# Moving the softmax normalisation, the weight conversions and one pre-addition inside an attention loop

## The chip, the cores and the metric

The kernel runs on one core of a Trainium2 chip. The metric is the device time of one execution in microseconds (us). TensorE (PE) multiplies, VectorE (DVE) and ScalarE (ACT) work elementwise, and most transfers are issued in order from the queue of SyncE (SP).

## The reference, cut to what matters

An attention with capped scores for 4 batches of 12 heads (448 tokens of 64 elements) is followed by a dense layer pair with squared ReLU (768 to 2048 to 768) on the 1792 tokens, and by a layer that sends each token to one of 8 experts.

```python
scores = scale * np.matmul(q, k.transpose(0, 1, 3, 2))
scores = cap * np.tanh(scores / cap)
scores = scores - np.max(scores, axis=-1, keepdims=True)
attn = np.exp(scores)
attn = attn / (np.sum(attn, axis=-1, keepdims=True) + 1e-09)
attn_out = np.matmul(attn, v)

h = x @ w_in            # x: 1792 x 768, from attn_out
r = np.maximum(h, 0.0)
x = (r * r) @ w_out
...
h = np.maximum(x[mask] @ w1[e], 0.0)      # per expert e
out[mask] = gate_w[mask, None] * (h @ w2[e])
```

## The kernel before, in words

The order of the work is written out by hand: each engine runs its instructions in the order in which the program emits them, and semaphores hold it where an operand or a buffer is not ready.

**Attention** (`attention`, L131) treats two heads at a time, a pair. There are 24 pairs and a loop of 25 periods (`pr` = 0 to 24, L297). In period `pr` TensorE computes the transposed scores of pair `pr` in three chunks of 128 keys (`scores`, L185), the values of the pair before (`values_last` L228, `values` L235 and L244), and the last 64 keys of the next pair (`scores_last`, L200), which ends the period on TensorE. ScalarE takes tanh of each score chunk (L191, L205) and exp of a pair in one instruction (L211), and copies the odd head's result out of PSUM (L253). VectorE does four kinds of things in a period, in this order: `fold` (L219), which adds exponentials of the pair before, chunk on chunk, into a tile `W`; the steps that are hung on the even index `i = 2*pr` (the middle slot); `prep` (L61 and L63), which splits the queries and keys of pair `pr + 2` into a high and a low part; `copy_out` of the even head (L256); and the steps that are hung on `i + 1` (the end slot).

**The row sums** come from matmuls with a matrix of ones (L244): one matmul for each head and each part, where the parts are `W` and the chunks that were not added into it. With `chunks = 2`, chunks 0 and 1 are added by one VectorE instruction and chunk 2 has ones matmuls of its own; with `chunks = 3` a second VectorE instruction adds chunk 2, and its matmuls fall away. Before, `chunks` is 3 in odd periods up to 15 and 2 elsewhere.

**The normalisation** goes over groups `u` of four heads (two periods). `norm_sum` (L274, L276) has SP send the row sums of a finished pair to a small tile `den` and then move the odd head's values into place (`x<-ot`), which must wait until the `den` transfer has read what it overwrites. `norm_recip` (L336, L337) takes the reciprocal on VectorE, `norm_spill` (L341) has SP write it to DRAM (`dd`), `norm_spread` (L349) has SP read it back, broadcast to all partitions (`r`, two transfers of 224 KB), and `norm_x` (L356) multiplies on VectorE, one instruction for each of the group's two pairs. The list `when` (L283) says at which index, counted from `i0 = 4u + 6`, each of the five steps is hung. An odd index is the end slot of a period, an even one the middle slot.

**The weights** for the first blocks of the dense layers come as 64-bit floats and are converted by VectorE in steps (`w_steps`, L445): three chunks, six VectorE steps each, of three kinds (begin, middle, end), plus two loads of 384 KB a chunk on SP's queue. Before, they hang on the indices 4, 5, 8, 9, 12, 13 and so on, two in every even period from 2 on. `split_x` (L403) splits group 0's normalised tokens for the first dense layer, one of six parts at each of six listed indices.

SP's queue takes in each period, in order: `qkraw` of pair `pr + 4` (L164, after `prep` has freed its buffer), the two `den` transfers, `x<-ot`, `v` (L170), and what the slots hang on it. Buffers: two for `qkraw`, `hl`, `W`, `r` and `den`, three for `ot`, four for `v`; in PSUM three for scores and two for values.

**At the start** SP loads the first queries and keys in two parts, then `cap`, values and the next pair. **After attention** the dense layers (`moe1`) and the experts (`moe2`) follow; from there on TensorE has work nearly all the time.

Of the kernel before, what the change touches and what calls it, by code (L numbers as in the profile page):

```python
# [21 lines left out]
NHD = B * H  # L22
# [12 lines left out]
FOLD_ALL = 32  # L35
FB = 2
NU = 4
# [11 lines left out]
class Kernel:  # L49
# [16 lines left out]
    def constants(self):  # L66
        nc, tc = self.nc, self.tc
        p = self.const
        cap = p.tile([128, 1], F32, name="cap")
        nc.sync.dma_start(out=cap, in_=self.a["cap"].rearrange("(o n) -> o n", o=1).to_broadcast([128, 1]))  # L70
        self.cap = cap

    def scales(self):
# [57 lines left out]
    def attention(self, tail_p):  # L131

        nc, tc, a = self.nc, self.tc, self.a
        with ExitStack() as ctx:
# [8 lines left out]
            ps_s = pool("pss", 3, space=PSUM)  # L143
            ps_o = pool("pso", 2, space=PSUM)

            z, y = self.ring["o"][0][0][:, :512], self.const.tile([128, 1], F32, name="y")
            nc.gpsimd.memset(y, 0.0)
            nc.scalar.activation(out=y, in_=y, func=ACTF.Tanh)
# [10 lines left out]
            def load(pr, cuts=(0, QK)):  # L159
                if pr < NP:  # L160
                    b, j = divmod(pr, H // 2)
                    raws[pr] = raw_p.tile([128, QK], F32, tag="qk", name="qkraw")
                    for c0, c1 in zip(cuts, cuts[1:]):
                        nc.sync.dma_start(out=raws[pr][:, c0:c1], in_=a["qk"][b, j, :, c0:c1])  # L164

            def load_v(pr):
                if pr < NP:
                    b, j = divmod(pr, H // 2)
                    vs[pr] = v_p.tile([KP, 2 * KC, D], F32, tag="v", name="v")
                    nc.sync.dma_start(out=vs[pr], in_=a["v"][b, j])  # L170
# [38 lines left out]
            def exps(pr):  # L209
                t = P[pr]  # L210
                nc.scalar.activation(out=t, in_=t, func=ACTF.Exp, scale=self.cap[:KP])  # L211

            def fold(pr, chunks):

                if chunks > 1:
                    W[pr] = w_p.tile([KP, 2, S], F32, tag="w", name="w")
                    src = P[pr][:, 0:2]
                    for c in range(1, chunks):
                        nc.vector.tensor_tensor(out=W[pr], in0=src, in1=P[pr][:, 2 * c:2 * c + 2], op=ALU.add)  # L219
                        src = W[pr]  # L220
# [36 lines left out]

            cuts = (0, S + KP, QK)
            load(0, cuts)
            self.constants()  # L260
            load_v(0)
            load(1)
            load_v(1)
# [16 lines left out]
            last = NHD // NU - 2  # L280
            for u in range(last + 1):
                i0 = NU * (u + 1) + 2
                when = (1, 1, 2, 5, 6)  # L283
                for j, f in zip(when, (
                    lambda u=u: self.norm_recip(den[u]),
                    lambda u=u: dd.update({u: self.norm_spill(den[u])}),
                    lambda u=u: r.update({u: self.norm_spread(n_p if u < last else tail_p, dd[u])}),
                    lambda u=u: self.norm_x(u, r[u], (0,)),
                    lambda u=u: self.norm_x(u, r[u], (1,)),
                )):  # L290
                    if u < last or j < 3:
                        steps.setdefault(i0 + j, []).append(f)


# [1 line left out]
            prep(1)  # L296
            for pr in range(NP + 1):  # L297
                i = 2 * pr
                chunks = 3 if pr % 2 == 1 and i < FOLD_ALL else 2
                if pr:  # L300
                    fold(pr - 1, chunks)
                for c in range(KC - 1):
                    if pr and c == KC - 2:
                        values_last(pr - 1)
                    if pr < NP:
                        scores(pr, c)
                    if not pr and not c:
                        scores_last(pr)
                if pr < NP:
                    exps(pr)  # L310
                if pr:
                    values(pr - 1, chunks)
                    copy_out(pr - 1, 1)
                scores_last(pr + 1)
                for f in steps.get(i, []) + self.side.get(i, []):
                    f()
                prep(pr + 2)
                if pr:
                    copy_out(pr - 1, 0)
                    if pr % 2:  # L320
                        p, bufs = (tail_p, 1) if pr == NP - 1 else (n_p, 2)
                        den.append(p.tile([128, NU * S // 128], F32, tag="den", name="den", bufs=bufs))
                else:
                    load(3)
                load(pr + 4)
                if pr:
                    norm_sum(i - 2)
                    norm_sum(i - 1)
                load_v(pr + 2)
                for f in steps.get(i + 1, []) + self.side.get(i + 1, []):  # L330
                    f()
# [429 lines left out]
def build(ctx, tc, a, stop=None):  # L761
    k = Kernel(ctx, tc, a)
    nc = tc.nc
    pool = lambda name, bufs=1, **kw: ctx.enter_context(tc.tile_pool(name=name, bufs=bufs, **kw))

    def xhl(p, g):
        n = GROUPS[g][1]
        k.xh[g] = p.tile([128, KD, n], F32R, name=f"xh{g}")
        k.xl[g] = p.tile([128, KD, n], F32R, name=f"xl{g}")

    with tc.manual_schedule():
        k.const = pool("const")
        k.cv_p = tc.alloc_tile_pool(name="cv", bufs=4, side="right")
        xp = tc.alloc_tile_pool(name="x", bufs=1, side="right")
        k.x = xp.tile([128, KD, NT], F32, name="x")
        k.raw_p = pool("wraw", 3)
        k.ring, k.used = {"i": [], "o": []}, {"i": 0, "o": 0}
        k.open_weights(pool("w0"), {"i": FB, "o": 1})
        k.xh, k.xl = [None] * NG, [None] * NG
        xhl(pool("x0"), 0)  # L780
        k.moe1_start()
        k.dram = pool("adr", 2, space=DRAM)
        tail_p = tc.alloc_tile_pool(name="tail", bufs=1, side="right")
        side = k.side = {6: [k.gate_loads]}
        at = iter([i for i in range(NU, NHD) if i % NU in (0, 1)])
        chunks = [k.w_steps(*c) for c in (("i", 0), ("i", 1), ("o", 0))]
        side[2] = [chunks[0][0]]
        for n, (_, *rest) in enumerate(chunks):
            for m, f in enumerate(rest):
                i = next(at)  # L790
                side.setdefault(i, []).append(f)
                if m == len(rest) // 2 and n + 1 < len(chunks):
                    side[i].append(chunks[n + 1][0])
        for j, i in enumerate((34, 35, 38, 39, 42, 43)):
            side.setdefault(i, []).append(lambda j=j: k.split_x(0, "dve", "dve", j))
        conv = k.w_conv(*k.chunk(0))
        side.setdefault(43, []).append(lambda: k.w_load(*k.chunk(0)))
        side[NHD] = [lambda: next(conv)]
        k.attention(tail_p)
        k.open_weights(pool("w1", reuse_waits="tile"), {"i": 1, "o": FB})  # L800
        x1 = pool("x1", reuse_waits="tile")
        for g in (1, 2, 3):
            xhl(x1, g)
        k.gt_p = pool("gt", reuse_waits="tile")
        with ExitStack() as c1:
            gp = c1.enter_context(tc.tile_pool(name="g", bufs=4, reuse_waits="tile"))
            k.g_p = gp
            k.ps_h = pool("psh", 3, space=PSUM, reuse_waits="tile")
            k.ps_y = pool("psy", 3, space=PSUM, reuse_waits="tile")
            k.ps_m = pool("psm", 2, space=PSUM, reuse_waits="tile")  # L810
            for j in range(KD):
                k.split_x(1, "act", "dve", j)
            late = {}

            def first():
                k.norm_recip(k.den_last)
                late["r"] = k.norm_spread(tail_p, k.norm_spill(k.den_last), "r2")
                for _ in conv:
                    pass
                k.w_split(*k.chunk(0))  # L820

            def second():
                k.norm_x(NHD // NU - 2, k.r_last)
                k.norm_x(NHD // NU - 1, late["r"])
                tail_p.release()
                for j in range(KD):
                    k.split_x(2, "act", "dve", j)

            k.moe1({(0, 0): first, (1, 0): second})
        xp.release()  # L830
        k.cv_p.release()
        k.h2_p = pool("h2")
        k.w2_p = pool("w2", 6)
        k.out_p = pool("o", 2)
        k.moe2()
        k.other_experts()
# [44 lines left out]
```

## Time and profile before

| | |
|---|---|
| median of 3 runs | 928.44 us (925.5 to 928.48) |
| profiled execution | 929.95 us, of which 928.2 us are the span from the first to the last instruction |
| PE, DVE, ACT busy | 97%, 62%, 40% of the span |
| mean granted TensorE clock | 0.986 |
| attention | about the first 193 us of the span |

A share of the span says little for a stage: attention, the dense layers and the experts load the engines differently. The attention's end is where the first matmul of the dense layer (L413) starts. Its periods can be counted on TensorE by the starts of L200, one per period.

### The profile page before, as it was taken

The numbers are of one execution on the slowest core, as the hardware profiler recorded it, in microseconds if no ns is written. First come the engines' busy times: TensorE is split into PE (matmuls) and PEld (weight loads), VectorE is DVE, ScalarE is ACT, GpSimd is POOL, SyncE is SP. The second block draws the span as 40 slices with busy tenths as digits, with TensorE's granted clock in tenths as the row PEclk, the third lists the DMA queues.
The fourth block names the chain that finished last, engine by engine and source line by source line (L and its number), as shares of the span: only waits on it lengthen the run. The fifth ranks groups of instructions, "written<-read, shape, count | busy, mean of one in ns | idle before, by whom it ended". The sixth has DMA issues, their size and how long they took to land.

```text
span 928.2 us, 12168 instructions
## 1 busy us (share of the span) xinstructions
PE 900.4 (97%) x4678; PEld 742.7 (80%) x4679; DVE 574.6 (62%) x1119; ACT 371.0 (40%) x532; POOL 0.8 (0%) x10
## 2 busy tenths in 40 slices
PE   8999899999999999999999999997889999999997
PEld 5555454568989889898898988986777998999997
DVE  5777586567857667676676766545566536426461
ACT  7999888956533223232232322334221111111111
POOL 0000000000000000000000000000000000000000
PEclk9999999999999999999999999999879999999999
DMA  5454555532312111121111211000114434526451
GB/s 196 136 166 116 170 150 145 150 105 60 101 51 67 53 52 53 50 68 52 52 56 47 68 51 35 1 1 0 58 46 120 119 115 124 156 83 171 136 162 47
DMA packets 39572, 83.30 MB, mean 90 GB/s; under 512 B 8656, under 2 KB 16976, under 8 KB 39504
## 3 DMA queue, kind: packets, MB, share of 16 engines
q1 hardware_dynamic: 35472, 76.92, 28.5%
q10 hardware_dynamic: 4032, 5.51, 1.6%
q8 instruction: 39, 0.64, 0.3%
q14 instruction: 29, 0.24, 0.1%
HBM read 73.97 MB, written 5.59 MB: 86 GB/s over the span
## 4 chain that ended last, share of the span: by engine, by line
PE 89%; DVE 5%; ACT 2%; DMA 2%; issue 1%; SPq 0%; DVEq 0%; ACTq 0%
PE h L413 12%; PE h L414 12%; PE h L415 12%; PE y L413 8%; PE y L415 8%; PE y L414 8%; PE o L235 5%; PE s L185 5%; PE o L413 4%; PE o L415 4%; PE o L414 4%; PE o L244 3%; PE o L228 2%; PE s L200 2%; DMA den<-ot 1%; DVE xl L63 1%
## 5 line engine op out<-in xcount | busy, mean ns | idle before, releaser
L413 PE MATMUL h<-xh,wih 128*128 128x512 f32 (+1 forms) x576 | 211.4, 367 | 0.0
L414 PE MATMUL h<-xl,wih 128*128 128x512 f32 (+1 forms) x576 | 210.6, 366 | 0.0
L415 PE MATMUL h<-xh,wil 128*128 128x512 f32 (+1 forms) x576 | 210.5, 365 | 0.0
L504 DVE TENSOR_TENSOR x<-y,x 128x512 f32<-128x512 f32 (+1 forms) x168 | 104.2, 623 | 72.3 <-PE y L415 71.1
L413 PE MATMUL y<-gh,woh 128*128 128x512 f32 (+1 forms) x384 | 141.6, 369 | 5.5 <-DVE x L504 5.3
L414 PE MATMUL y<-gl,woh 128*128 128x512 f32 (+1 forms) x384 | 140.3, 365 | 0.0
L415 PE MATMUL y<-gh,wol 128*128 128x512 f32 (+1 forms) x384 | 140.1, 365 | 0.0
L480 ACT ACTIVATE r<-h 128x512 f32<-128x512 f32 (+1 forms) x64 | 34.9, 546 | 245.6 <-PE h L415 239.0
L413 PEld LDWEIGHTS h<-xh,wih 128*128 128x128 f32 x576 | 109.7, 190 | 12.3 <-issue 0.7
L414 PEld LDWEIGHTS h<-xl,wih 128*128 128x128 f32 x576 | 109.7, 190 | 11.4
L415 PEld LDWEIGHTS h<-xh,wil 128*128 128x128 f32 x576 | 109.5, 190 | 11.6
L413 PEld LDWEIGHTS y<-gh,woh 128*128 128x128 f32 x384 | 72.7, 189 | 15.3 <-DVE x L504 6.6
L415 PEld LDWEIGHTS y<-gh,wol 128*128 128x128 f32 x384 | 72.7, 189 | 8.3
L414 PEld LDWEIGHTS y<-gl,woh 128*128 128x128 f32 x384 | 72.8, 190 | 7.6
L486 DVE TENSOR_TENSOR gl<-r,gh 128x512 fp32r<-128x512 f32 (+1 forms) x64 | 39.7, 620 | 61.5 <-ACT gh L485 61.3
L413 PE MATMUL o<-w2h,hh 128*128 128x384 f32 x224 | 75.0, 335 | 0.0
L415 PE MATMUL o<-w2h,hl 128*128 128x384 f32 x224 | 74.9, 334 | 0.0
L414 PE MATMUL o<-w2l,hh 128*128 128x384 f32 x224 | 74.9, 334 | 0.0
L191 ACT ACTIVATE t<-s,tscale 128x896 f32<-128x896 f32 x72 | 70.1, 1008 | 8.0 <-PE s L185 6.8
L211 ACT ACTIVATE t<-t,cap 128x3136 f32<-128x3136 f32 x24 | 69.8, 2910 | 0.8
L185 PE MATMUL s<-hl 64*128 64x448 f32 x432 | 64.5, 421 | 0.1
L680 DVE SCALAR_TENSOR_TENSOR hl<-h,hh 128x512 fp32r<-128x512 f32 (+1 forms) x32 | 19.9, 623 | 65.4 <-ACT hh L679 65.4
(119 smaller groups left out, 1035.8 us busy)
## 6 DMA issues: line engine op xcount, KB each, us to landing
raw<-w SPq DMA_DIRECT2D x64, 384.0 KB, 3.2
raw<-w_in SPq DMA_DIRECT2D x32, 384.0 KB, 3.1
raw<-w_out SPq DMA_DIRECT2D x32, 384.0 KB, 3.1
qkraw<-qk SPq DMA_DIRECT2D x23, 480.0 KB, 4.2
v<-v SPq DMA_DIRECT2D x24, 256.0 KB, 2.9
r<-dd SPq DMA_DIRECT2D x24, 224.0 KB, 3.9
out<-o ACTq DMA_DIRECT2D x28, 192.0 KB, 1.9
x<-ot SPq DMA_DIRECT2D x24, 112.0 KB, 2.2
```

What stands on the lines that cost most here:

```text
L185: nc.tensor.matmul(out=s[:, h, :S], lhsT=w[rows[h], kp, S + c * KP:S + (c + 1) * KP], rhs=w[rows[h], qp, :S], start=n == 0, stop=n == 2,)
L191: nc.scalar.activation(out=P[pr][:, 2 * c:2 * c + 2], in_=s[:, :, :S], func=ACTF.Tanh, scale=self.tscale[:KP])
L211: nc.scalar.activation(out=t, in_=t, func=ACTF.Exp, scale=self.cap[:KP])
L235: nc.tensor.matmul(out=o[h][rows[h]], lhsT=v[:, 2 * c + h], rhs=p[:, 2 * c + h], start=False, stop=c == KC - 2,)
L244: nc.tensor.matmul(out=o[h][rows[1 - h]], lhsT=one, rhs=t[:, h], start=False, stop=n == len(parts) - 1)
L413: nc.tensor.matmul(out=out, lhsT=wh, rhs=vh, start=first and j == 0, stop=False)
L414: nc.tensor.matmul(out=out, lhsT=wh, rhs=vl, start=False, stop=False)
L415: nc.tensor.matmul(out=out, lhsT=wl, rhs=vh, start=False, stop=last and j == m - 1)
L480: nc.scalar.activation(out=r, in_=ps, func=ACTF.Relu)
L486: split = lambda: nc.vector.tensor_tensor(out=gl, in0=r, in1=f32(gh), op=ALU.subtract)
L504: nc.vector.tensor_tensor(out=y, in0=ps, in1=y, op=ALU.add)
L680: nc.vector.scalar_tensor_tensor(out=hl, in0=ps, scalar=0.0, in1=f32(hh), op0=ALU.max, op1=ALU.subtract)
```

## The change

Four edits to the order of the work in attention; what is computed stays the same.

- `cap` (0.5 KB) is loaded from ScalarE's queue at the top of `attention`, no longer from SP's queue between the first loads.
- The normalisation steps move back: reciprocal and spill from `i0 + 1` to `i0 + 2` (end slot of one period to the middle slot of the next), the broadcast read from `i0 + 2` to `i0 + 3` (the end slot of the same period), both multiplications from `i0 + 5` and `i0 + 6` to `i0 + 8` (the middle slot three periods after the reciprocal's). The last full group takes `i0 + 7`.
- `chunks` is 3 in every period up to 15, not in the odd ones alone.
- The weight steps hang on 5, 7, 9 and so on: one in each period's end slot. The `split_x` parts move from 34 to 43 to 36 to 45.

```diff
-        nc.sync.dma_start(out=cap, in_=self.a["cap"].rearrange("(o n) -> o n", o=1).to_broadcast([128, 1]))
+        nc.scalar.dma_start(out=cap, in_=self.a["cap"].rearrange("(o n) -> o n", o=1).to_broadcast([128, 1]))
...
             ps_o = pool("pso", 2, space=PSUM)
 
+            self.constants()
             z, y = self.ring["o"][0][0][:, :512], self.const.tile([128, 1], F32, name="y")
...
             load(0, cuts)
-            self.constants()
             load_v(0)
...
-                when = (1, 1, 2, 5, 6)
+                when = (2, 2, 3, 8, 8) if i0 + 8 <= NHD else (2, 2, 3, 7, 7)
...
-                    if u < last or j < 3:
+                    if u < last or j < 4:
...
-                chunks = 3 if pr % 2 == 1 and i < FOLD_ALL else 2
+                chunks = 3 if i < FOLD_ALL else 2
...
-        at = iter([i for i in range(NU, NHD) if i % NU in (0, 1)])
+        at = iter(range(NU + 1, NHD, 2))
...
-        for j, i in enumerate((34, 35, 38, 39, 42, 43)):
+        for j, i in enumerate((36, 40, 41, 43, 44, 45)):
```

## Rows read from the trace of the kernel before

**Rows 1.** The page, part 1: busy us of each engine, share, instructions

```profile
PE 900.4 (97%) x4678; PEld 742.7 (80%) x4679; DVE 574.6 (62%) x1119; ACT 371.0 (40%) x532; POOL 0.8 (0%) x10
```

**Rows 2.** Stretches of attention: length, busy PE PEld DVE ACT POOL, clock, DMA, GB/s

```profile
26.00:84.00 58.00, 58.00 (x351) 29.90 (x347) 42.26 (x67) 55.65 (x50) 0.00 (x0) 1.00 0.53 147
84.00:126.00 42.00, 37.34 (x213) 18.82 (x212) 29.12 (x46) 33.23 (x30) 0.00 (x0) 0.96 0.50 147
126.00:164.80 38.80, 37.90 (x226) 18.88 (x225) 28.96 (x50) 35.20 (x31) 0.00 (x0) 1.00 0.54 155
```

**Rows 3.** Timeline of PE: start us, length us, line, operation [idle before, releaser]

```profile
18.91 0.86 PE L200 MATMUL s<-hl 128*128 128x448 f32 x3
...
26.40 0.88 PE L200 MATMUL s<-hl 128*128 128x448 f32 x3
...
33.16 0.87 PE L200 MATMUL s<-hl 128*128 128x448 f32 x3
...
116.61 1.32 PE L244 MATMUL o<-w,one 128*64 128x448 f32 x4 [2.37 <-DVE w L219]
...
125.76 0.87 PE L200 MATMUL s<-hl 128*128 128x448 f32 x3
...
164.76 0.88 PE L200 MATMUL s<-hl 128*128 128x448 f32 x3
```

**Rows 4.** Waits from 84 to 164 us: total us, times, longest us

```profile
DVE x L356 <- DMA r<-dd: 14.3, 5, 5.1
...
DVE den L336 <- DMA den<-ot: 4.2, 5, 1.0
```

**Rows 5.** Chain that ended last, 108 to 118 us: start, us, what

```profile
112.16 2.85 DMA den<-ot
...
115.61 0.96 DVE w L219
```

**Rows 6.** Timeline of ACT: an exp and the copy behind it

```profile
73.91 2.91 ACT L211 ACTIVATE t<-t,cap 128x3136 f32<-128x3136 f32 x1
76.73 0.51 ACT L253 COPY ot<-o 128x448 f32<-128x448 f32 x1
```

**Rows 7.** Stretches of two periods each, columns as in rows 2

```profile
47.52:61.77 14.25, 14.25 (x87) 7.35 (x87) 11.40 (x18) 13.66 (x13) 0.00 (x0) 1.00 0.56 162
...
107.88:125.86 17.98, 15.61 (x87) 7.77 (x85) 10.72 (x18) 13.30 (x13) 0.00 (x0) 0.91 0.47 136
```

**Rows 8.** DVE groups from 20 to 125 us: shapes xcount | busy, mean ns | idle

```profile
L219 DVE TENSOR_TENSOR w<-w,t 128x896 f32<-128x896 f32 x7 | 7.6, 1092 | 0.2
L356 DVE TENSOR_TENSOR x<-x,r 128x448 f32<-128x448 f32 x10 | 6.2, 618 | 13.7 <-DMA r<-dd 13.7
```

**Rows 9.** Timeline of SP's queue: start, issue us, line, transfer

```profile
61.31 0.56 SPq L274 DMA_DIRECT2D den<-x  x1
...
71.86 0.39 SPq L341 DMA_DIRECT2D dd<-den  x1
74.25 1.30 SPq L349 DMA_DIRECT2D r<-dd  x2
...
76.24 0.55 SPq L274 DMA_DIRECT2D den<-x  x1
```

**Rows 10.** Timeline of DVE: the copy whose row sums the last of rows 9 sends

```profile
69.93 0.62 DVE L256 COPY x<-o 128x448 f32<-128x448 f32 x1
```

**Rows 11.** The page, part 6: transfer, count, KB each, median us to landing

```profile
r<-dd SPq DMA_DIRECT2D x24, 224.0 KB, 3.9
```

**Rows 12.** The load of cap on SP's queue

```profile
1.71 0.42 SPq L70 DMA_DIRECT2D cap<-cap  x1
```

**Rows 13.** Stretches at the start, columns as in rows 2

```profile
6.00:9.00 3.00, 2.28 (x15) 1.17 (x14) 0.45 (x4) 2.72 (x5) 0.00 (x0) 1.00 0.97 379
...
11.50:14.50 3.00, 3.00 (x15) 2.46 (x16) 2.83 (x3) 3.00 (x4) 0.00 (x0) 0.50 0.76 237
```

**Rows 14.** The stretch right after attention, columns as in rows 2

```profile
193.00:200.00 7.00, 7.00 (x33) 5.80 (x32) 4.99 (x9) 5.92 (x11) 0.00 (x0) 1.00 0.35 82
```

## The prediction, made blind

> **What bounds the kernel now.** I read the busy shares first: TensorE is busy 97% of the span [rows 1], so only a stage in which it waits, or work taken off it, can move the time. All four edits lie in attention, so I cut attention into stretches. From 26 to 84 us TensorE never idles; from 84 to 126 us it is busy 37.34 of 42.00 us and from 126 to 164.8 us 37.90 of 38.80 us [rows 2]. Then I counted periods on TensorE. An even period, with ones matmuls for two parts, lasts 26.40 - 18.91 = 7.49 us, an odd one, with one part, 33.16 - 26.40 = 6.76 us [rows 3]; call them 7.50 and 6.75. Periods 2 to 15 run from 18.91 to 125.76 us, 106.85 us for seven of each kind, which need 7 x 14.25 = 99.75: **7.1 us are lost**. Periods 16 to 20 (all 7.50) run to 164.76 us, 39.0 for 37.5: **1.5 us are lost** [rows 3].
>
> Who loses it? The waits from 84 to 164 us show VectorE waiting 14.3 us for the broadcast reciprocals and 4.2 us for the row sums [rows 4]. The chain shows the order: a `den` transfer that takes until 115.0 us, the reciprocal behind it, the addition into W, and only then TensorE's L244 [rows 5], which had idled 2.37 us [rows 3]. So VectorE stands in `norm_x` and `norm_recip`, and `fold`, which TensorE needs, is queued behind them. The transfers are late because SP is: the row sums that VectorE's copy at 69.93 us completes are sent at 76.24 us [rows 9, 10], a lag of 76.24 - 70.55 = 5.7 us. SP's two-period cycle is 76.24 - 61.31 = 14.93 us against TensorE's 14.25, and in it SP stands from 72.25 to 74.25 us between `dd` and the read of `r` [rows 9], waiting for `dd` to land.
>
> **The change part by part.**
>
> *Third chunk pre-added* (periods 2, 4 ... 14). Each drops its second part's ones matmuls, 7.50 - 6.75 = 0.75 us of TensorE; seven times, 5.25 us. It adds one VectorE addition of 1.09 us [rows 8] to each. VectorE is busy 11.40 of 14.25 us in a full pair of undisturbed periods, weight steps included [rows 7]; 11.40 + 1.09 = 12.5 us must fit 13.5, and does. W itself is safe: from a period's start VectorE does the copy (0.62), at most one weight step (under 1.5, an estimate: three instructions of about half a microsecond) and two additions (2.2), 4.3 us, while L244 is due about 5.9 us in (6.75 less its 0.85). ScalarE is nearer: its busy time is 13.66 us in two periods [rows 7], 6.83 each. Where its copy finds PSUM ready it starts 76.73 - 73.91 = 2.82 us after an exp of 2.91 us [rows 6], so the floor is about 6.83 - 0.09 = 6.74. Short periods in a row have no slack on ScalarE and none is seen in this trace, so I bound a period by 6.75 and 6.83: over 14 periods the gain is 5.25 to 99.75 - 14 x 6.83 = 4.1 us; I take the middle, **4.7**.
>
> *Normalisation steps moved back.* No instruction is added; eleven `dd` transfers, 22 reads of `r`, the reciprocals and twenty-odd multiplications move. Three things follow. First, the reciprocal and the multiplications now stand behind `fold` in VectorE's queue, so what still waits there holds up only `prep` and the even head's copy. `prep` is due a period later; the copy is needed by L228, which comes behind the next period's first two score chunks, about 2 us on (an estimate). Second, a multiplication has 2.5 periods (16.9 us) after its read's place in the program instead of 1.5. The read lands about 5 us after SP starts to issue it (1.30 for two issues [rows 9] and 3.9 to landing [rows 11]), which leaves some 7 us for SP's lag even after SP's other transfers. The reciprocal has, by the same reckoning, 5 to 6 us for a lag of 5.7 seen. Third, `dd` and the read are now parted by `qkraw`, both `den`, `x<-ot` and `v`, so that the 2.0 us that SP stood still are covered: 14.93 - 2.0 = 12.9 us, under the new 13.5. Behind the read's two issues (1.3 us) now stand the next period's `qkraw` and `den`, as before. I let nearly all stalls go: of 8.6 us, **8.1**, bounds 4.3 (half remain) and 8.6. Part of it is the clock: the stretch around the worst stall has 0.91 over 17.98 us [rows 7], 0.09 x 17.98 = 1.6 us of lost full-speed time, after the 2.37 us idle.
>
> On that the Trainium skill, page "TensorE: Matmul & The Clock Gate", section Part 1, says that a throttled clock is the default that activity releases, and that its phase differs from run to run, so the same gap need not cost the same. By that rule some 1.6 us of the stalls could be absent from another execution of the kernel before, and the gain would be 11.5 instead of 13.1.
>
> *Weight steps one per period.* The same 18 steps, moved later by up to five periods. They even out VectorE's load: before, two fell in one period. The loads of the second and third chunk move from the ends of periods 4 and 10 to the ends of 5 and 11; on SP they come behind `v` as before. Worth nothing of its own. The `split_x` parts move two to four indices later, into periods that have no second addition; the last still comes two periods before its first reader. Nothing.
>
> *cap on ScalarE's queue.* SP's issue of 0.42 us [rows 12] goes from in front of the values and of pair 1, for which TensorE waits at 9 to 11 us. ScalarE issues it while it has nothing else to do. But from 6 to 9 us the DMA engines are busy 0.97 [rows 13], so an earlier issue needn't land as much earlier. Bounds: a loss of 0.3 (ScalarE's table load starts later) and a gain of 0.5; I take **0.3**. The half-speed stretch behind it (clock 0.50 from 11.5 to 14.5 us [rows 13], 1.5 us lost) could go too if the gap shrinks, which only the low end of the range counts.
>
> The Trainium skill, page "DMA: Bandwidth & Descriptors", section "Issuing engines are not separate DMA queues", says that issuing from another engine saves only the sequencer's time to issue, since all transfers share the same engines. By it this part is worth 0.42 us at most, and the total 13.2 rather than 13.1.
>
> *The end.* Group 9's two multiplications (0.62 each [rows 8]) now come after the last copy, ahead of the split of the next tokens; VectorE is busy 4.99 of 7.00 us there and TensorE all of it [rows 14], with a whole group's matmuls before the split is read. Nothing; without that cover 1.2.
>
> **Sum:** 4.7 + 8.1 + 0.3 = 13.1 us off the profiled execution's 929.95 (1.75 of it outside the span): **916.8 us**. The median of the runs is 1.5 us lower; whether that is stalls that differ between executions can't be told, so the low end takes it in.
>
> **The rivals.**
>
> *ScalarE holds the periods.* If short periods in a row cost as much as the pair does now, 7.1 us each, the 4.7 us don't come: 921.5. For it: 6.83 us busy in a 6.75 us period. Against: an odd period already ends in 6.76.
>
> *SP stays the clock.* If its cycle stays at 15.0 us (copies of row sums slow down behind the reads), seven pairs lose 7 x 1.5 = 10.5 us, of which a lag of about 5 is absorbed as it is now: 5.5 later, 922.3. For it: SP's cycle is already longer than TensorE's. Against: the 2.0 us it stands still are in it. Both rivals together: 927.0.
>
> *The waits stay and VectorE becomes the bound*, the case on the other side. VectorE's work of 12.1 us (the mean of 11.40 and 10.72 [rows 7], plus 1.09) plus the longest waits seen, 5.1 + 1.0 us [rows 4], is 18.2 us for two periods; seven pairs take 127.4 instead of 106.85, so 929.95 + 20.5 = 950. It is slower than now from waits of 106.85 / 7 - 12.1 = 3.2 us a pair. For it: an added 1.09 us stands in front of the steps. Against: each wait's transfer has half to one and a half periods more.
>
> **How the numbers follow.** Forecast 0.69, ScalarE 0.10, SP 0.10, both 0.06, VectorE slower 0.05. This kernel's measurement can tell about 0.5%, 4.6 us. So faster (under 923.8) 0.89, same 0.06, slower 0.05. The low end is the upper bounds of all parts with the median's 1.5 and the clock's 1.5: 929.95 - 5.25 - 8.6 - 0.5 - 1.5 - 1.5 = 912.6; call it 912.3. The high end takes in both single rivals: 923.0.
>
> **What would show it.** In the trace after: period starts of L200 6.75 to 6.83 us apart for periods 1 to 15 and 7.50 after; no wait of TensorE for W and hardly one of VectorE for `r`; TensorE busy all of 84 to 160 us; the first L413 near 180 us instead of 193; no clock below 1.00 after 20 us within attention. Wrong would be: L253 or L191 named before TensorE's waits in every period (ScalarE), a `den` or `qkraw` wait of several microseconds (SP), L219 late again (VectorE), or a stage after attention that gives the time back.

## The result, and the profile after

The changed kernel takes 914.15 us (median of 4 runs, 913.67 to 915.08) against 928.46 (925.5 to 931.51) for the kernel before: a ratio of 0.9847, 95% interval 0.9814 to 0.988. The profiled execution took 914.05 us with a span of 912.3 us, 15.9 less than the 929.95 of before.

Where they went can be read from one matmul. These are the first L413 of before and of after (timeline of TensorE: start us, length us, line, operation):

```profile
192.98 0.50 PE L413 MATMUL h<-xh,wih 128*128 128x512 f32 x1
```

```profile
180.48 0.50 PE L413 MATMUL h<-xh,wih 128*128 128x512 f32 x1
```

Attention ends 12.5 us earlier. The rest of the span is 735.22 us before and 731.82 after, 3.4 us less, though nothing was changed there. Those 3.4 us lie in the 60 us where the dense layers hand over to the experts (stretches as in [rows 2]; first before, then after):

```profile
632.98:692.98 60.00, 48.32 (x204) 40.79 (x205) 35.94 (x98) 16.03 (x32) 0.00 (x0) 0.86 0.10 34
```

```profile
620.48:680.48 60.00, 48.11 (x220) 40.32 (x221) 38.82 (x107) 16.70 (x33) 0.00 (x0) 0.91 0.13 40
```

TensorE is busy equally long, 48.3 and 48.1 us, but at a granted clock of 0.86 in one execution and 0.91 in the other. The clock is at 0.50 for 17.1 of these 60 us before and for 10.2 after; half of the difference is 3.4 us.

**The periods.** The starts of L201 (L200 before), one per period, from the timeline of TensorE after; the counterpart of [rows 3]:

```profile
27.04 0.47 PE L201 MATMUL s<-hl 128*128 128x448 f32 x1
...
33.78 0.47 PE L201 MATMUL s<-hl 128*128 128x448 f32 x1
...
114.74 0.47 PE L201 MATMUL s<-hl 128*128 128x448 f32 x1
...
152.26 0.68 PE L201 MATMUL s<-hl 128*128 128x448 f32 x2
```

From 27.04 to 114.74 us thirteen periods of 6.746 us follow one another (before, 6.75 and 7.50 in turn), and the five behind them take 37.52 us, the bare 5 x 7.50 that they need without a wait. The stretches of [rows 2 and 7] after:

```profile
26.00:84.00 58.00, 58.00 (x355) 30.64 (x353) 49.05 (x75) 57.40 (x53) 0.00 (x0) 1.00 0.56 160
84.00:126.00 42.00, 42.00 (x260) 21.93 (x258) 36.37 (x58) 41.05 (x38) 0.00 (x0) 1.00 0.61 175
126.00:150.00 24.00, 24.00 (x145) 12.02 (x145) 17.86 (x32) 22.42 (x20) 0.00 (x0) 1.00 0.61 160
47.38:60.87 13.49, 13.49 (x83) 7.07 (x83) 11.74 (x18) 13.34 (x13) 0.00 (x0) 1.00 0.56 176
94.61:108.10 13.49, 13.49 (x83) 7.07 (x84) 12.50 (x20) 13.34 (x13) 0.00 (x0) 1.00 0.62 194
```

TensorE is busy all of 26 to 150 us at full clock; from 84 to 126 us it had been 37.34 of 42.00 at 0.96. ScalarE is now the fullest engine beside it, 13.34 of 13.49 us, with VectorE at 11.74 to 12.50. TensorE's need of 6.75 us a period and the floor of 6.74 that the prediction read for ScalarE lie too close for the period's length to tell which of the two holds it; from 27 to 114 us neither is seen to wait for the other. The waits from 84 to 164 us after, against [rows 4]:

```profile
DVE x L257 <- PE o L245: 13.2, 10, 2.1
...
DVE den L336 <- DMA den<-ot: 0.5, 1, 0.5
```

The 14.3 us for the reciprocals `r` have no line any more, and neither has any wait of TensorE for W. VectorE now waits for TensorE instead.

**SP's queue** after, over two periods (timeline: start, issue us, line, transfer), against [rows 9], and the same transfer one and two cycles on:

```profile
69.53 0.40 SPq L341 DMA_DIRECT2D dd<-den  x1
70.02 0.38 SPq L165 DMA_DIRECT2D qkraw<-qk  x1
70.49 0.52 SPq L274 DMA_DIRECT2D den<-x  x1
71.10 0.54 SPq L274 DMA_DIRECT2D den<-ot  x1
74.59 0.52 SPq L276 DMA_DIRECT2D x<-ot  x1
75.20 0.54 SPq L171 DMA_DIRECT2D v<-v  x1
75.83 1.30 SPq L349 DMA_DIRECT2D r<-dd  x2
...
84.39 0.52 SPq L274 DMA_DIRECT2D den<-x  x1
...
99.66 0.52 SPq L274 DMA_DIRECT2D den<-x  x1
...
114.19 0.52 SPq L274 DMA_DIRECT2D den<-x  x1
```

Before, SP stood still between `dd` and the read of `r`; now five transfers lie between them and the read goes out as soon as its turn comes. What SP still stands for, 2 to 4 us ahead of each `x<-ot`, was there before as well. Its first cycle here is 84.39 - 70.49 = 13.9 us, the two behind it 15.3 (a weight load comes in) and 14.5: on average 14.6 us, 1.1 over the 13.49 that TensorE takes for two periods.

**The start** went the other way. The first instruction of VectorE on the first queries and keys, before and after (timeline of VectorE; the bracket is the idle time ahead and what ended it):

```profile
3.76 0.46 DVE L61 CAST hl<-qkraw 128x576 fp32r<-128x576 f32 x1 [2.24 <-DMA qkraw<-qk]
```

```profile
5.18 0.46 DVE L61 CAST hl<-qkraw 128x576 fp32r<-128x576 f32 x1 [3.67 <-DMA qkraw<-qk]
```

It came 1.4 us later. Both executions also have 3.4 us at half clock in the start (11.3 to 14.7 us before, 14.8 to 18.2 after), so the two can be compared. Below, "attention proper" is the time from VectorE's first copy of values (19.02 us before, 20.41 after) to the first L413: 174.0 us before, 160.1 after. That leaves the start out.

### The profile page after: what moved, and what is told of

It is laid out like the page before. It is cut to its first block, busy times and chain, and to the rows that moved or that the text cites. A ratio compares the mean times of both kernels' runs of the same rounds, so it can differ in the third digit from the quotient of the medians.

```text
span 912.3 us, 12124 instructions
## 1 busy us (share of the span) xinstructions
PE 889.0 (97%) x4650; PEld 736.6 (81%) x4651; DVE 581.4 (64%) x1126; ACT 368.8 (40%) x532; POOL 0.8 (0%) x10
## 4 chain that ended last, share of the span: by engine, by line
PE 92%; DVE 5%; ACT 2%; DMA 0%; issue 0%; DVEq 0%
PE h L413 12%; PE h L414 12%; PE h L415 12%; PE y L413 8%; PE y L415 8%; PE y L414 8%; PE o L236 6%; PE s L186 5%; PE o L413 4%; PE o L415 4%; PE o L414 4%; PE o L245 3%; PE o L229 2%; PE s L201 2%; DVE xl L63 1%; ACT xh L57 1%
## 5 line engine op out<-in xcount | busy, mean ns | idle before, releaser
L413 PE MATMUL h<-xh,wih 128*128 128x512 f32 (+1 forms) x576 | 210.2, 365 | 0.0
L413 PE MATMUL y<-gh,woh 128*128 128x512 f32 (+1 forms) x384 | 141.4, 368 | 5.7 <-DVE x L504 5.5
L413 PEld LDWEIGHTS h<-xh,wih 128*128 128x128 f32 x576 | 109.0, 189 | 12.0 <-issue 0.7
L414 PEld LDWEIGHTS h<-xl,wih 128*128 128x128 f32 x576 | 108.9, 189 | 11.3
L415 PEld LDWEIGHTS h<-xh,wil 128*128 128x128 f32 x576 | 108.8, 189 | 11.3
L413 PEld LDWEIGHTS y<-gh,woh 128*128 128x128 f32 x384 | 72.6, 189 | 15.6 <-DVE x L504 6.9
L413 PE MATMUL o<-w2h,hh 128*128 128x384 f32 x224 | 75.1, 335 | 0.0
L236 PE MATMUL o<-t,v 128*64 128x448 f32 x288 | 60.4, 555 | 0.0
```

Source lines behind the costliest of these rows:

```text
L236: nc.tensor.matmul(out=o[h][rows[h]], lhsT=v[:, 2 * c + h], rhs=p[:, 2 * c + h], start=False, stop=c == KC - 2,)
L413: nc.tensor.matmul(out=out, lhsT=wh, rhs=vh, start=first and j == 0, stop=False)
L414: nc.tensor.matmul(out=out, lhsT=wh, rhs=vl, start=False, stop=False)
L415: nc.tensor.matmul(out=out, lhsT=wl, rhs=vh, start=False, stop=last and j == m - 1)
```

## The experiments

The kernel before took 927.5 to 927.6 us (medians) beside these runs; ratios are to it. The first four isolate edits or undo one.

**Only the third chunk** (the kernel before with one line changed):

```diff
-                chunks = 3 if pr % 2 == 1 and i < FOLD_ALL else 2
+                chunks = 3 if i < FOLD_ALL else 2
```

> The kernel before with the third chunk pre-added in all periods up to 15, nothing else changed. Theory A, the moved normalisation steps are what lets the shorter periods come: VectorE still stands ahead of fold in its waits for the transfers, SP's cycle of two periods stays near 15 us, so periods 2 to 15 still take 14.5 to 15.5 us a pair (101.5 to 108 us against 106.85 before), attention ends between 188 and 194 us, time 924 to 930. Theory B, the parts add up independently: 5.3 us less, end at 187.7, stalls as before (8.6 us), time 923. Theory C, VectorE becomes the bound: 18.2 us a pair with the longest waits, end at 213, time 949.

926.01 us, ratio 0.9977 (0.9956 to 0.9997); attention proper 174.6 us, as theory A had it. TensorE drops the second part's ones matmuls of the same seven periods as in the full change, and in this trace all of it is given back. From the timeline of TensorE in this run:

```profile
116.58 1.76 PE L244 MATMUL o<-w,one 128*64 128x448 f32 x4 [5.21 <-DVE w L219]
```

The wait for W of [rows 3] has grown from 2.37 to 5.21 us, and another of 3.51 us stands at 67.65 us. In all TensorE idles 9.5 us of attention proper, 6.3 before; the rest of what is given back is the clock, at 0.50 for two stretches of 6.8 us, one from each of these waits on, where the kernel before has one of 3.4. Shorter periods do not make SP's transfers come sooner.

**Only the normalisation** (the kernel before with two lines changed):

```diff
-                when = (1, 1, 2, 5, 6)
+                when = (2, 2, 3, 8, 8) if i0 + 8 <= NHD else (2, 2, 3, 7, 7)
...
-                    if u < last or j < 3:
+                    if u < last or j < 4:
```

> The kernel before with the normalisation steps moved, nothing else changed. Theory A, all the stalls came from these steps' places: the 8.6 us lost in periods 2 to 20 go, attention ends at 193.0 - 8.6 = 184.4 us, time 919.5 to 920.5; SP's lag (row sums sent after the copy that completes them) falls below 4 us in the second half. Theory B, the uneven weight steps (two in an even period) are needed for it too: half of the stalls stay, end at 188 to 189, time 924. In both no wait of TensorE for W of over 1 us is left by A and some by B.

917.45 us, ratio 0.9895 (0.9863 to 0.9927); attention proper 165.4 us, which is 174.0 less the 8.6 of stalls that the prediction had counted. One mark of theory A was missed: the lag of SP (from the end of VectorE's copy to the issue of its row sums) still reaches 5.2 us, though TensorE waits for nothing behind it. Attention from 20 to 180 us, before and here (stretches):

```profile
20.00:180.00 160.00, 154.44 (x915) 78.46 (x913) 112.95 (x181) 144.19 (x127) 0.00 (x0) 0.99 0.50 142
```

```profile
20.00:180.00 160.00, 159.24 (x957) 81.05 (x957) 116.51 (x187) 151.02 (x132) 0.00 (x0) 1.00 0.55 151
```

**Both, without the moved weight steps and with cap as before** (the two diffs above together):

> The kernel before with the normalisation steps moved and the third chunk pre-added; weight steps and group 0's split at their old indices, cap on SP. Theory A, the weight steps' move is worth nothing: 14 periods of 6.75 us, no stall, attention ends where it does with cap on SP and everything else changed, 179 us, time 912.5 to 914. Theory B, with 12.5 us of 13.5 the load must be even: a period with two weight steps and two additions (0.62 + 1.5 + 2.2 + 0.9 + 0.5 + 1.8 = 7.5 us) overruns 6.75, the copy comes up to 0.8 us late, still inside the 2 us that L229's predecessors leave, but the lag adds up over neighbouring periods and 1 to 4 us of stalls come back: end at 180 to 183.

912.88 us, ratio 0.9847 (0.9814 to 0.988); attention proper 161.7 us. The third chunk is worth 917.45 - 912.88 = 4.6 us here, against 1.5 alone: the edits don't add, because the periods can only get shorter once VectorE isn't held. "No stall" was not quite met: SP's lag grows to 7.8 us, TensorE waits 1.1 us for `v`, and two periods are 1.1 and 0.5 us too long.

**cap back on SP's queue** (the changed kernel):

```diff
-        nc.scalar.dma_start(out=cap, in_=self.a["cap"].rearrange("(o n) -> o n", o=1).to_broadcast([128, 1]))
+        nc.sync.dma_start(out=cap, in_=self.a["cap"].rearrange("(o n) -> o n", o=1).to_broadcast([128, 1]))
...
-            self.constants()
...
             load(0, cuts)
+            self.constants()
```

> The changed kernel with cap back on SP's queue between the first loads; all else as changed. In the changed kernel the first part of the queries and keys lands at 5.16 us (3.74 before) and the end of period 1 (VectorE's first copy of a result) comes at 20.41 us instead of 19.02. Theory A, cap's transfer on a second queue slows the first loads: the first part lands near 3.7 us, the copy comes at 19.0, attention ends (first L413) at 180.48 - 1.4 = 179.1 us. Theory B, the late start was chance of that execution: landing and end stay spread between the two whatever queue cap is on, and a start near 5.2 us can show up here too. In the whole time 1.4 us is 0.15%, so the stretch decides, not the time: about 912.8 us by A, 914.2 by B.

913.25 us, ratio 0.9846 (0.9817 to 0.9876), so the time as a whole doesn't tell cap's two places apart. The trace does: the first part is used at 3.69 us instead of 5.18, and the first L413 comes at 178.44 us instead of 180.48 (attention proper 160.8). Not all of these 2.04 us can be put down to cap: this execution has no stretch at half clock in its start. Of the seven kernels with cap on SP's queue four have none (first copy at 17.53 to 18.22 us) and three have one (19.02 to 21.32). With cap first on ScalarE's queue the one start without such a stretch has its copy at 20.09 us, the three with one at 20.41 to 20.54. From 2 to 3.5 us, with cap on SP's queue and then in the changed kernel (stretches; the last two columns are the DMA share and GB/s):

```profile
2.00:3.50 1.50, 1.50 (x5) 1.12 (x4) 0.00 (x0) 0.27 (x2) 0.00 (x0) 1.00 0.89 291
```

```profile
2.00:3.50 1.50, 1.50 (x5) 1.12 (x4) 0.00 (x0) 0.70 (x2) 0.00 (x0) 1.00 0.33 100
```

With cap on ScalarE's queue the first loads run at a third of the rate. The count of packets says with what they share the transfer engines: with cap on SP's queue 279 packets start in this stretch, all of SP's queue; in the changed kernel 65 of SP's queue beside 59 of ScalarE's, which are cap's pieces of 4 bytes.

This run and the one before it differ by the places of the weight steps and of `split_x` alone: 913.25 against 912.88 with overlapping runs, so the times show no worth of these. Attention proper is 0.9 us shorter here (160.8 against 161.7), in one execution of each; one wait of TensorE of 0.4 us is left, with SP's lag at up to 7.3 us.

The next three put parts of the normalisation's move back. The disputed question: does the gain come from standing behind `fold`, so that a late transfer no longer holds W up, or from SP, whose cycle gets shorter when `dd` and the read of `r` are parted?

**The read right behind `dd` again** (the changed kernel):

```diff
-                when = (2, 2, 3, 8, 8) if i0 + 8 <= NHD else (2, 2, 3, 7, 7)
+                when = (2, 2, 2, 8, 8) if i0 + 8 <= NHD else (2, 2, 2, 7, 7)
```

> The changed kernel with the broadcast read of r hung in the same middle slot as the reciprocal and its spill, so that on SP it follows dd directly again and SP stands until dd has landed (2.0 us before the change). All else as changed. From the first result copy to the first L413 the changed kernel takes 160.1 us (the same copy with only the normalisation moved: 165.4; before: 174.0). Theory A, the places behind fold and the longer distances are what count: 160 to 161.5 us, no TensorE wait for W, time 914 to 915. Theory B, it is SP's cycle: SP stands 2 us a pair again, its cycle of about 15 us is over the 13.5 that TensorE now needs, the lag grows by 1.5 us a pair past the 5 to 6 us that the reciprocal and qkraw can bear: 164 to 168 us, time 918 to 922.

925.6 us, ratio 0.9977 (0.9957 to 0.9996); attention proper 170.5 us, worse than both theories. Moving one transfer one slot earlier takes back 10.4 of the 13.9 us. SP's queue (timeline) and what stood in it from 20 to 165 us (waits of SP: total us, times, longest us):

```profile
72.42 0.40 SPq L341 DMA_DIRECT2D dd<-den  x1
74.84 1.30 SPq L349 DMA_DIRECT2D r<-dd  x2
```

```profile
SPq L276 <- DMA den<-x: 44.0, 19, 4.0
SPq L349 <- DMA dd<-den: 20.4, 8, 3.9
```

The 2.0 us between issues are back, 20.4 us in eight reads, and SP falls up to 10.7 us behind VectorE's copies. The reciprocal and both multiplications still stand behind `fold`, and no wait for W is seen; the time is lost elsewhere, to the row sums (19.1 us of VectorE's waits for `den<-ot`) and to values that come late (timeline of TensorE):

```profile
99.65 0.99 PE L229 MATMUL o<-t,v 64*128 64x448 f32 x3 [0.96 <-DMA v<-v]
...
117.34 1.87 PE L229 MATMUL o<-t,v 64*128 64x448 f32 x4 [3.94 <-DMA v<-v]
```

Of the 10.4 us, TensorE idles 6.6, and its clock is at 0.50 for 6.8 us around the second of these waits. So the place behind `fold` alone is not enough while SP's cycle is longer than the loop's.

**Only the multiplications late** (the changed kernel, reciprocal, spill and read as before):

```diff
+                when = (1, 1, 2, 8, 8) if i0 + 8 <= NHD else (1, 1, 2, 7, 7)
```

> The changed kernel with reciprocal, spill and read at their old indices (1, 1, 2), so that only the multiplications come later. Theory A, the reciprocal's wait for the row sums in front of fold is the stall that reaches TensorE (the chain before the change names it last): VectorE's waits for r vanish, those for den grow to over 10 us in total, TensorE waits 4 us or more for W, first copy to first L413 takes 165 to 171 us, time 919 to 925. Theory B, the multiplications' waits (14.3 of the 18.5 us) were the cause and den's only followed from them: 160 to 162 us, time 914 to 916.

924.57 us, ratio 0.9967 (0.9949 to 0.9984); attention proper 170.7 us: theory A. From 20 to 165 us the waits of VectorE and TensorE are

```profile
DVE den L336 <- DMA den<-ot: 16.9, 7, 4.3
...
PE o L245 <- DVE w L220: 7.0, 3, 3.1
```

VectorE no longer waits for `r`, yet TensorE waits for W: the reciprocal, in front of `fold`, waits for row sums that SP sends late. The wait has only moved from one step to the other.

**Read parted, reciprocal in front of `fold`** (the changed kernel):

```diff
+                when = (1, 1, 3, 8, 8) if i0 + 8 <= NHD else (1, 1, 3, 7, 7)
```

> The changed kernel with reciprocal and spill at their old index (in front of fold) and only the read and the multiplications moved; against the kernel with only the multiplications moved (924.57 us, 170.7 us from first copy to first L413) only the read's place differs: one slot later, behind the next x<-ot and v. Theory A, parting the read from dd is the main thing: SP no longer stands 2 us a pair, lag 6 us at most, 160 to 163 us, time 914 to 917. Theory B, the reciprocal must leave the front of fold: VectorE waits there for den as before, TensorE waits 4 us or more for W, 165 us or more, time 919 or more.

918.05 us, ratio 0.9895 (0.9874 to 0.9916); attention proper 164.2 us, between what the two theories gave. Against the run before, the read alone has moved: 170.7 - 164.2 = 6.5 us. To the changed kernel 4.1 us are left: one wait for W of 2.4 us, and 3.4 us at half clock behind it, which cost 1.7. So parting the read is the larger part, about 6.5 of 10.6, and the reciprocal's place is the rest. The split depends on the order: without the parting the reciprocal's place is worth 170.7 - 170.5 = 0.2 us, and with the reciprocal behind `fold` the parting is worth 10.4.

**SP relieved in another way**: the kernel before, normalisation untouched, with the loads of `v` from pair 2 on issued by GpSimd:

```diff
-                    nc.sync.dma_start(out=vs[pr], in_=a["v"][b, j])
+                    (nc.gpsimd if pr > 1 else nc.sync).dma_start(out=vs[pr], in_=a["v"][b, j])
```

> The kernel before with the loads of v inside the loop (pair 2 on) issued from GpSimd's queue instead of SP's; nothing else changed, the normalisation in its old places. Theory A, SP's cycle of two periods is what made the stalls: it loses two issues of v, 2 x 0.6 us, from 14.9 to 13.7 us, under TensorE's 14.25, so the lag (5 to 9 us from period 6 on before) stays under 4 us, most of the 8.6 us of stalls go, first copy to first L413 165.5 to 168 us instead of 174.0, time 918 to 921. Theory B, the transfers themselves are what is slow (DMA engines half busy in bursts), and who issues them is nothing: lag and stalls as before, 172 to 175 us, time 926 to 928.

919.61 us, ratio 0.9908 (0.9889 to 0.9927); attention proper 166.6 us, 7.4 less than before. SP still stands between `dd` (71.94 us) and the read (74.19 us), and every step of VectorE has its old place; of SP's issues only the 2 x 0.53 us of `v` in two periods are gone. With them go 3.0 us that SP stood for `v`'s buffers from 20 to 165 us, and its standing ahead of the read shrinks from 18.2 to 13.7 us, while that ahead of `x<-ot` grows from 45.4 to 55.2. The waits of VectorE for `r` fall from 18.8 to 2.5 us. SP's lag stays within 5.6 us (8.9 before); theory A had asked for under 4. This is the most direct evidence that SP's cycle was the cause, since nothing of the normalisation moved. Moving `v` also takes its data out of SP's queue, so that SP's other transfers stand behind less; that was not separated from the shorter issue.

**cap issued later from ScalarE** (the changed kernel):

```diff
-            self.constants()
...
             nc.scalar.activation(out=y, in_=y, func=ACTF.Tanh)
+            self.constants()
```

> The changed kernel with cap still on ScalarE's queue but issued behind the first tanh (near 2.3 us instead of 0.78). Theory A, cap's small packets beside the first loads slow those down: the first part of the queries and keys lands near 3.7 us as with cap on SP (3.5 to 3.7 in four such kernels, 5.16 with cap first on ScalarE's queue), cap lands near 6 us, the first result copy comes at 17.5 to 19.1 us, time 912.5 to 913.5. Theory B, any transfer from a second queue slows them or it was chance: landing at 4.5 us or later, copy at 19.5 to 20.5, time near 914.

911.95 us, ratio 0.9832 (0.9804 to 0.986); attention proper 160.1 us. The late issue that was meant did not come about (timeline of ScalarE):

```profile
0.78 1.28 ACT L148 ACT_TABLE_LOAD   x1 [0.65 <-PEq L873]
0.92 0.38 ACTq L70 DMA_DIRECT2D cap<-cap  x1
2.08 0.20 ACT L148 ACTIVATE y<-y 128x1 f32<-128x1 f32 x1
```

The transfer stands behind the tanh in the program and was issued 1.16 us ahead of it. It moved from 0.78 to 0.92 us, just behind SP's first issue at 0.79 instead of beside it, and the first part was used at 4.27 us, between 3.69 and 5.18. The packets fit the loss being cap's: from 2 to 3 us only 7 of them start and the loads run at 253 GB/s, as with cap on SP's queue (257); from 3 to 4.5 us 120 of them start beside 79 of SP's queue, at 69 GB/s (164 with cap on SP's queue). `v` and the next pair's loads were issued as early here as in the changed kernel, so their earlier issue is not what slows the loads from 2 us on. A cap issued well after the first part's landing wasn't measured.

**Where the new limit lies.** The third chunk in all periods up to 23, with cap on SP's queue as above:

```diff
-FOLD_ALL = 32
+FOLD_ALL = 48
```

> The changed kernel with cap on SP and the third chunk pre-added in periods 16 to 23 as well. TensorE drops 0.75 us in eight periods, 6.0 us; VectorE gets eight more additions of 1.09 us beside the six parts of group 0's split. Theory A, VectorE holds 13.5 us a pair with them too (worst period: copy 0.6, weight step 1.5, two additions 2.2, reciprocal 0.4, split 1.1, prep 1.8 = 7.5 us, made up in the next): first copy to first L413 154 to 155 us, time 907 to 908. Theory B, VectorE is the bound there: half of the gain is lost, 157 to 158 us, time 910.

908.92 us (906.14 to 914.2), ratio 0.9786 (0.9753 to 0.9819). Its runs spread over 8 us, and the profiled one is the slowest of them, with 159.0 us of attention proper: there SP lags 5 to 8 us from period 12 on, TensorE waits 1.91 us for `v` at 118.89 us, in the first of the added short periods, and its clock is at 0.50 for 3.4 us from 120.2 us. The lag has been built up by the short periods before, and with short periods to the end it stays at 5 to 7 us for the next five. This trace meets neither theory: VectorE is not what TensorE waits for.

**All of it together**: the changed kernel with cap's issue at 0.92 us, the third chunk up to 23 and `v` on GpSimd's queue:

> The kernel with cap behind the first tanh on ScalarE's queue (160.1 us from first copy to first L413), with the third chunk pre-added in periods 16 to 23 too (alone it took 159.0, with SP's lag at 5 to 8 us from period 12 on and TensorE waiting for v and late copies) and the loop's v loads on GpSimd's queue. Theory A, SP's lag was what cost e8 its gain: lag under 4 us, 22 periods of 6.75 us, 154 to 155 us, time 905.5 to 907. Theory B, VectorE is the bound once the third addition meets the split's parts: lag falls but periods 17 to 22 stay at 7.0 to 7.8 us, 157 us, time 908.5.

908.31 us (907.0 to 908.79), ratio 0.979 (0.9775 to 0.9806): the lowest median here, with a narrow spread. Attention proper is 154.5 us, as theory A had it, though the time is nearer to theory B's. The two periods in which VectorE has most to do read (stretches)

```profile
121.28:134.78 13.50, 13.50 (x83) 7.09 (x84) 13.19 (x22) 13.35 (x13) 1.08 (x3) 1.00 0.62 178
```

TensorE is full, and VectorE with 13.19 and ScalarE with 13.35 of 13.50 us leave little for a further step; SP's lag is at most 5.0 us.

## Why the prediction was right

It gave 916.8 us (912.3 to 923.0); 914.15 was measured, and the profiled execution's 914.05 splits into its terms.

- **Third chunk:** 4.7 taken, 5.3 came (14 x (7.125 - 6.745)). TensorE's 6.75 and the floor read from one exp and the copy behind it, 6.74, are what the periods then took; the rival "ScalarE holds the periods" fell. The bound of 6.83 came from a pair of periods in which ScalarE's instructions partly stood apart: the same thirteen are busy 13.66 us there and 13.34 us where they follow closely.
- **Stalls:** 8.1 taken, all 8.6 came; the normalisation alone shows them, 174.0 to 165.4. That no clock below 1.00 would be left in the loop held too, so the clock's share came with the idle time.
- **SP's cycle:** 12.9 us predicted, 13.9, 15.3 and 14.5 measured one after the other. This step was mis-sized: parting the read saves 2.0 us, but the new order lets more of the standing ahead of `x<-ot` show (52.4 us from 20 to 165 us, 45.4 before). The cycle is still longer than the loop's 13.5, as the rival "SP stays the clock" had it, so the lag grew to 5.7 us by period 13 and shrank again once periods were 7.50. What saved the sum was the other claim, that the reciprocal bears 5 to 6 us: it did, with nothing to spare (VectorE waits 0.5 us for `den` once), and it is luck that the short periods end after fourteen, before the lag outgrows it. With cap on SP's queue the lag reached 7.3 us, and 7.8 with the weight steps at their old places, and 0.7 and 1.6 us were lost in long periods. That rival was nearer than its 0.10.
- **Weight steps:** nothing predicted, 0.4 us the other way between two medians with overlapping runs, 0.9 us of attention proper in single traces: not told apart from nothing.
- **cap:** +0.3 predicted, -1.4 in the trace. The step that failed took the issue of 0.42 us as all that was at stake and bounded the loss by ScalarE's table load. What was lost is the rate of the first loads, and the half-speed stretch that the low end hoped to lose stayed, only later. All four kernels with cap first on ScalarE's queue use the first part at 5.15 to 5.29 us, all seven with cap on SP's at 3.54 to 3.95, the two with cap just behind at 4.27 and 4.66. On this the Trainium skill, page "DMA: Bandwidth & Descriptors", section "Issuing engines are not separate DMA queues", says that another issuing engine saves only the sequencer's time. As a ceiling on the gain that held; the measurement adds that the sign may turn. For `v` the measurement is 7.4 us, from 1.06 us less of issue in two periods and the waits that went with it, on a queue whose cycle was longer than the loop's.
- **Outside attention:** 0 predicted, 3.4 came, which the clock accounts for (17.1 us at 0.50 before, 10.2 after). The Trainium skill, page "TensorE: Matmul & The Clock Gate", section Part 1, says that the clock's phase differs between runs; 0.86 and 0.91 over the same code agree. Before's profiled execution lay 1.5 us above its median, and its 735.2 us behind attention are the longest of all thirteen traces (730.8 to 733.8 in the others), so part of the 3.4 belongs to that execution. Why the medians differ by 14.3 (13.4 from the 927.5 of the later runs) where attention gives 12.5 stays open.

Together: 13.1 + 0.6 + 0.5 - 1.7 + 3.4 = 15.9, the whole difference. The forecast was right by its two large terms; the two small errors, cap and the clock, had opposite signs, and the clock's 3.4 us are no part of the mechanism: without them the difference is 12.5, against 13.1 forecast.

The rival of VectorE as the new bound fell as well: its steps no longer wait at all for `r`, and it stands 13.2 us waiting for TensorE.

## What to carry to other kernels

When an engine waits for a transfer, read the issuing queue's own cycle against the loop's before moving the waiting step: here a queue at a DMA share of 0.50 set the pace, since it stood for its own transfers. A read parted from what it depends on (6.5 us, or 10.4 with the reciprocal behind `fold`) or one load on another queue (7.4 us) moved the end, while waiting steps moved without that left attention proper at 170.5 to 170.7 of 174.0 us. Part a transfer from one that depends on it by other transfers of the same queue. Removing work from the busiest engine paid fully only after that (1.5 us before, 4.6 after), so the order in which edits are tried decides what they seem to be worth.

## What the runs showed of the hardware

- A transfer of 0.5 KB, issued on a second queue at the same moment as the first load (0.78 us both), left the transfers at 100 to 108 GB/s from 2 to 3.5 us (four kernels) where they otherwise ran at 285 to 304 (seven); the first part came into use 1.4 us later. In that stretch 59 packets of 4 bytes from the one queue start beside 65 from the other. Why a packet of 4 bytes takes so much of the rate is open; a small transfer of another form was not tried.
- ScalarE's queue issued a transfer at 0.92 us that follows in the program a table load running until 2.06 us and a tanh at 2.08. An instruction's place in the program did not delay an issue that waits for nothing.
- Neighbouring instructions of ScalarE overlap: behind an exp of 2.91 us the copy starts after 2.82 us. The same thirteen instructions of two periods are busy 13.66 us where some wait [rows 7] and 13.34 us where all follow closely.
